# Attention on one Trainium2 core: the weighted sums in runs of three key blocks, the next minimum and exponential ahead of the evictions

## Chip, cores and metric

The kernel runs on one core of a Trainium2 chip. The metric is the device time of one execution in microseconds (us), lower is better. An execution of the kernel before takes 633.66 us (median of three: 632.58, 633.66 and 633.7).

## What is computed

Three stages follow each other: an attention whose mask comes from hash buckets, a mixture of experts, and a mixer. The change lies in the attention alone:

```python
q_bits = (np.einsum('bhsd,dk->bhsk', q, proj) > 0)          # 6 bits, the same for k
mask = q_bucket[:, :, :, None] == k_bucket[:, :, None, :]
scores = scale * np.matmul(q, k.transpose(0, 1, 3, 2))       # 2 x 8 heads, 768 x 768, head size 64
scores = np.where(mask, scores, -1000000000.0)
scores = scores - np.max(scores, axis=-1, keepdims=True)
attn = np.exp(scores)
attn = attn / (np.sum(attn, axis=-1, keepdims=True) + 1e-09)
return np.matmul(attn, v)
```

The attention's output is the token matrix (2 x 768 x 512) that the experts and then the mixer read.

## The kernel before

The sixteen heads are taken as eight pairs. A **unit** `u` is one head's block of 128 query rows against all 768 keys. There are 96 units (`NU`), six to a **group** `g = u // 6` (three query blocks times two heads of a pair); below `w = u % 6` is the unit's place in its group and `h = u % 2` its head. Units 0 to 23 (`NP2`) go through an older loop; the loop of this change goes over units 22 to 95.

What one unit does, by function:

- `scores(u)`: four TensorE matmuls of the operand tile `op` into a score tile `ps` (two buffers in PSUM), L242. The mask is part of the operands.
- `low(u)`: on VectorE (DVE) the scores are moved from `ps` to a tile `sc` (three buffers) with their minimum, L249.
- `expo(u)`: on ScalarE (ACT) the exponential of `sc` in place, with the row sum, L256.
- `transp(u)`: six TensorE transposes of `sc`, three into each of two PSUM tiles `pst` (a pool of two buffers, so the next unit's first three transposes need this unit's first tile, and its next three the second), L270. Two evictions take them to `pt`, the transposed weights of the group: the first half on ACT (L282), the second half on ACT in the odd units (set `relieve`) and on DVE (L284) in the even ones.
- `av(g, kb)`: the weighted sums of a whole group over key block `kb`: two matmuls, one for each head, which write 64 rows each of `pav` (L295; in the profile each is two instructions). `av_out(g)` moves the finished `pav` to `xT` on ACT (L302) and takes the reciprocal of the row sums on DVE (L304, L305).
- `av_tok(g)` turns `xT` into token rows (px, L312, and three or four DVE operations).

The order of each engine's queue is the order in which the program is written (`manual_schedule`), and each engine takes its queue in that order. In the loop, unit `u` is written as: `scores(u + 2)`; in an odd unit of groups up to 14 two `av` of the group before (so key blocks 0 and 1 in w = 1, 2 and 3 in w = 3, 4 and 5 in w = 5); in w = 5 also `av_out`; then `transp(u)`, in which `low(u + 2)` is written after the first half's eviction and `expo(u + 2)` after the second's; then `av_tok` where one is due (w = 1), and the side work planned for that unit: halving 64-bit weights to 32 bits on DVE (`narrow`, L592, L594, L596, in five units of six up to unit 73), splitting the next pair's operands on GpSimd (POOL, L174 to L181), and loads. The last group (units 90 to 95) has its own places for `av`: there two runs of three key blocks stand already.

Of the kernel before, what the change touches and what calls it, by code (L numbers as in the profile page):

```python
# [59 lines left out]
def attention(tc, nc, cst, cbf, cst_src, tri_src, cw, qkT, vt, iw_src, route, wide, errands, xh, early):  # L60
    with ExitStack() as ctx:
# [139 lines left out]
        NU = len(units)  # L201
# [3 lines left out]
        NP2 = 24  # L205
# [25 lines left out]
        def scores(u):  # L231
            i, half, qb, h = units[u]
            op = opnd[i]
            g = u // 6
            if u % 6 == 0:
                sums[g] = sm_p.tile([128, 6], F32, name="sum")
                mns[g] = sm_p.tile([128, 6], F32, name="mn")
            ps = ps_s.tile([128, 2, 512], F32, name="ps")
            c0 = 384 * half + 128 * qb
            for x, kk in ((0, 128), (2, 76)):  # L240
                for n in range(2):
                    nc.tensor.matmul(ps[:, n, :384], lhsT=op[:kk, h, x, c0:c0 + 128],  # L242
                                     rhs=op[:kk, h, x + 1, 384 * n:384 * n + 384], start=(x == 0), stop=(x == 2))
            pss[u] = ps

        def low(u):
            g, w = u // 6, 2 * units[u][2] + units[u][3]
            sc = sc_p.tile([128, S], F32, name="sc")
            nc.vector.tensor_scalar(sc.rearrange("p (a b) -> p a b", a=2), pss.pop(u)[:, :, :384], NEG, None,  # L249
                                    op0=ALU.min, op1=ALU.min, accum_out=mns[g][:, w:w + 1])  # L250
            scs[u] = sc

        def expo(u):
            g, w = u // 6, 2 * units[u][2] + units[u][3]
            sc = scs[u]
            nc.scalar.activation(sc, sc, AF.Exp, bias=mns[g][:, w:w + 1], scale=-1.0,  # L256
                                 accum_out=sums[g][:, w:w + 1])

        def transp(u):
            _, _, qb, h = units[u]  # L260
            g = u // 6
            if u % 6 == 0:
                pts[g] = [pt_p.tile([128, NB, 384], F32, name=f"pt{x}") for x in range(2)]
            sc = scs.pop(u)
            pt = pts[g][h]
            for n in range(2):
                ps = ps_t.tile([128, 512], F32, name="pst")
                for j in range(3):
                    kb = 3 * n + j
                    nc.tensor.transpose(ps[:, 128 * j:128 * j + 128], sc[:, 128 * kb:128 * kb + 128], ident)  # L270
                dst = pt[:, 3 * n:3 * n + 3, 128 * qb:128 * qb + 128]
                src = ps[:, :384].rearrange("p (a b) -> p a b", a=3)
                if u < NP2 - 2 and h == 1:
                    if n == 0:
                        low(u + 2)
                        nc.vector.tensor_copy(dst, src)
                    else:
                        expo(u + 2)
                        nc.scalar.activation(dst, src, AF.Copy)
                    continue  # L280
                if n == 0 or u in relieve:
                    nc.scalar.activation(dst, src, AF.Copy)  # L282
                else:
                    nc.vector.tensor_copy(dst, src)  # L284
                if n == 0 and u + 2 < NU:
                    low(u + 2)
            if u + 2 < NU and (u >= NP2 - 2 or h == 0):
                expo(u + 2)

        def av(g, kb, q0=0, q1=3):  # L290
            if kb == 0 and q0 == 0:
                pav[g] = ps_a.tile([128, 512], F32, name="pav")
            sl = slice(128 * q0, 128 * q1)
            for h in range(2):
                nc.tensor.matmul(pav[g][64 * h:64 * h + 64, sl], lhsT=vtile[g // 2][:, kb, 64 * h:64 * h + 64],  # L295
                                 rhs=pts[g][h][:, kb, sl], start=(kb == 0), stop=(kb == NB - 1))

        def av_out(g, q0=0, q1=3):
            if q0 == 0:
                xTs[g] = sm_p.tile([128, 384], F32, name="xT", bufs=2)  # L300
            sl = slice(128 * q0, 128 * q1)
            nc.scalar.activation(xTs[g][:, sl], pav[g][:, sl], AF.Copy)  # L302
            rs = sums[g][:, 2 * q0:2 * q1]
            nc.vector.tensor_scalar(rs, rs, 1e-9, None, op0=ALU.add)  # L304
            nc.vector.reciprocal(rs, rs)  # L305

        def av_tok(g, between=None):
            i, half = g // 2, g % 2
            b, p = pairs[i]
            px = px_tile()[:, :438].rearrange("p (t c) -> p t c", t=3)  # L310
            for x in range(3):
                nc.tensor.matmul(px[:, x], lhsT=xTs[g][:, 128 * x:128 * x + 128], rhs=iw[:, p], start=True, stop=True)  # L312
            inv = sums[g].rearrange("p (t h) -> p t h", t=3).unsqueeze(3)
            X, L = route.tiles(b)
            t = slice(3 * half, 3 * half + 3)
            lg = sm_p.tile([128, 3, 2, 9], F32, name="lg", bufs=2)
            nc.vector.tensor_tensor(lg, px[:, :, 128:].rearrange("p t (h e) -> p t h e", h=2),
                                    inv.to_broadcast([128, 3, 2, 9]), op=ALU.mult)
            Lh = L[:, t, :]
            if p == 0:  # L320
                nc.vector.tensor_tensor(Lh, lg[:, :, 0], lg[:, :, 1], op=ALU.add)
            else:
                nc.vector.tensor_tensor(Lh, Lh, lg[:, :, 0], op=ALU.add)
                nc.vector.tensor_tensor(Lh, Lh, lg[:, :, 1], op=ALU.add)
            if between is not None:
                between()
            nc.vector.tensor_tensor(
                X[:, t, 128 * p:128 * p + 128].rearrange("p t (h d) -> p t h d", h=2),
                px[:, :, :128].rearrange("p t (h d) -> p t h d", h=2),
                inv.to_broadcast([128, 3, 2, 64]), op=ALU.mult)  # L330
# [174 lines left out]
        for p in range(NP2 // 2 - 1):  # L505
            g, w = p // 3, p % 3
            scores2(p + 1)
            transp(2 * p)
            if g >= 1:
                av(g - 1, 2 * w)  # L510
                av(g - 1, 2 * w + 1)
                if w == 2:
                    av_out(g - 1)
            transp(2 * p + 1)
            for u in (2 * p, 2 * p + 1):
                for x in tok.get(u, ()):
                    av_tok(x)
                for f in todo.pop(u, ()):
                    f()
        for u in range(NP2 - 2, NU):  # L520
            g, w = u // 6, u % 6
            last = g == NG - 1
            if u + 2 < NU:
                scores(u + 2)
            if g >= 1 and not last and w % 2 == 1:
                av(g - 1, w - 1)
                av(g - 1, w)
            if w == 5 and g >= 1 and not last:
                av_out(g - 1)
            if last and w == 1:  # L530
                for kb in range(3, NB):
                    av(g - 1, kb)
                av_out(g - 1)
            if last and w in (2, 4):
                q = w // 4
                for kb in range(NB):
                    av(g, kb, q, q + 1)
                av_out(g, q, q + 1)
            transp(u)
            if last and w == 0:  # L540
                for kb in range(3):
                    av(g - 1, kb)
            for x in tok.get(u, ()):
                av_tok(x)
            for f in todo.pop(u, ()):
                f()
# [3 lines left out]
        g = NG - 1  # L550
# [860 lines left out]
def build(tc, nc, a):  # L1411
    with ExitStack() as ctx:
# [45 lines left out]
        with tc.tile_pool(name="xtok", bufs=1, side="right") as xp:  # L1458
            route = Router(nc, tc, cst, cbf, rp, xp, xs, ys)
            zt = []  # L1460

            def zero(e):
                if not zt:
                    zt.append(wr_a.tile([128, 2048], F32, name="wr"))
                    nc.gpsimd.memset(zt[0][:, :1024], 0.0)
                nc.sync.dma_start(xs[CAP * e:CAP * e + CAP].rearrange("(p r) d -> p (r d)", r=2), zt[0][:, :1024])

            errands = [lambda e=e: zero(e) for e in range(E)] + [lambda: wload(0), lambda: wload(1)]
            x0 = attention(tc, nc, cst, cbf, a["cst"], a["tri"], cw, a["qkT"], a["vt"], a["iw"], route, wide, errands,
                           xh, early)  # L1470
# [67 lines left out]
```

## Time and profile before

| | |
|---|---|
| median of three executions | 633.66 us |
| the profiled execution | 636.94 us |
| its span, first to last instruction | 635.1 us |
| TensorE (PE) busy | 620.9 us, 98% |
| DVE busy | 402.7 us, 63% |
| ACT busy | 351.4 us, 55% |
| POOL busy | 256.8 us, 40% |
| units 24 to 89 (first transposes at 68.75, last at 228.62) | 159.9 us |

Times inside the span are counted from its first instruction. PE's line shows matmuls; PEld, its weight loads, runs beside them. Ends of matmuls are modelled, so what PE's work costs is read from the distance between the starts of successive groups. A bracket behind a row gives the idle time before it and what ended that.

### The profile page before, as it was taken

The page shows a single profiled execution, that of the slowest core. Times are in us where ns is not written, and L with a number is a line of the kernel's source. Part 1 is how long each engine was busy: PE and PEld are TensorE (multiplying, and loading weights), DVE is VectorE, ACT ScalarE, POOL GpSimd, SP SyncE. Part 2 cuts the span into 40 slices and gives each one's busy share as a digit, 9 for nine tenths or more (in the row PEclk, how much of TensorE's full clock was granted, in tenths as well). Part 3 has the DMA queues.
Part 4 walks back from the last instruction along what each step waited for, and adds up shares of the span by engine and source line. Part 5 has one row for each costly group of instructions (what it writes and reads, how often), then busy time and mean ns, then how long its engine had stood idle before and what let it go on. Part 6 is the DMA issues. An engine that isn't in the chain of part 4 may idle for free. (4 is left out here: it accounts for less than half of the span.)

```text
span 635.1 us, 10543 instructions
## 1 busy us (share of the span) xinstructions
PE 620.9 (98%) x4028; PEld 498.2 (78%) x4028; DVE 402.7 (63%) x740; ACT 351.4 (55%) x643; POOL 256.8 (40%) x191
## 2 busy tenths in 40 slices
PE   8999999999989999999999999999999999999997
PEld 4666676766657767889889989989788888788896
DVE  5667788879777657737786646544456876854252
ACT  5757667767657756445455545544657457533220
POOL 2252140422340241444355453355456676774320
PEclk9999999999989999999999999999999999999999
DMA  7349999786945101788868798855223322321012
GB/s 241 102 138 279 288 297 293 194 207 220 250 141 138 50 0 64 244 322 278 309 216 299 242 326 298 261 209 183 85 84 113 103 100 84 116 84 66 35 34 100
DMA packets 51828, 112.57 MB, mean 177 GB/s; under 512 B 4112, under 2 KB 13984, under 8 KB 51776
## 3 DMA queue, kind: packets, MB, share of 16 engines
q1 hardware_dynamic: 48416, 97.73, 48.9%
q10 hardware_dynamic: 1440, 7.86, 3.6%
q0 software_dynamic: 1920, 6.29, 3.0%
q8 instruction: 32, 0.52, 0.3%
q14 instruction: 20, 0.16, 0.1%
HBM read 74.06 MB, written 22.54 MB: 152 GB/s over the span
## 5 line engine op out<-in xcount | busy, mean ns | idle before, releaser
L249 DVE TENSOR_SCALAR_CACHE_REDUCE sc<-ps 128x768 f32<-128x768 f32 x96 | 90.7, 953 | 29.1 <-PE ps L242 14.5
L1263 PE MATMUL acc<-wt,z 128*128 128x256 f32 (+1 forms) x576 | 106.4, 340 | 0.6 <-DVE z L1249 0.5
L1263 PEld LDWEIGHTS acc<-wt,z 128*128 128x128 f32 x576 | 90.5, 188 | 15.8 <-DVE z L1249 1.4
L848 POOL TENSOR_TENSOR whl<-wr,whl 128x1024 fp32r<-128x1024 f32 x30 | 72.1, 2425 | 69.6 <-ACT whl L846 62.8
L256 ACT ACTIVATE sc<-sc,mn 128x768 f32<-128x768 f32 x96 | 89.7, 936 | 14.2 <-DVE sc L249 12.7
L921 PE MATMUL mph<-xhl,whl 128*128 128x256 f32 x768 | 94.2, 284 | 0.4 <-DVE xhl L584 0.3
L921 PEld LDWEIGHTS mph<-xhl,whl 128*128 128x128 f32 x768 | 93.1, 192 | 1.3 <-DVE xhl L584 0.5
L270 PEld LDWEIGHTS pst<-cst,sc 128*128 128x128 f32 x576 | 64.1, 141 | 35.4 <-ACT sc L256 14.4
L282 ACT ACTIVATE pt<-pst 128x384 f32<-128x384 f32 x132 | 59.6, 488 | 51.1 <-PE pst L270 47.8
L270 PE MATMUL pst<-cst,sc 128*128 128x128 f32 x576 | 83.0, 280 | 3.2 <-ACT pt L282 3.1
L937 PE MATMUL mpy<-whl,h 128*128 128x512 f32 x336 | 79.4, 392 | 0.0
L295 PE MATMUL pav<-pt,v 128*64 128x384 f32 (+1 forms) x432 | 74.3, 468 | 0.0
L846 ACT ACTIVATE whl<-wr 128x1024 fp32r<-128x1024 f32 x64 | 64.0, 1051 | 15.4 <-PE mpy L937 6.5
L937 PEld LDWEIGHTS mpy<-whl,h 128*128 128x128 f32 x336 | 62.1, 188 | 12.3
L242 PE MATMUL ps<-op 128*128 128x384 f32 (+1 forms) x288 | 68.6, 360 | 0.5 <-DVE sc L249 0.5
L242 PEld LDWEIGHTS ps<-op 128*128 128x128 f32 (+1 forms) x288 | 47.2, 190 | 3.5 <-issue 2.5
L616 POOL TENSOR_TENSOR wt<-wr,wt 128x768 fp32r<-128x768 f32 x24 | 45.8, 1927 | 8.9 <-issue 3.9
L295 PEld LDWEIGHTS pav<-pt,v 128*64 128x64 f32 x432 | 26.4, 137 | 27.9 <-issue 27.7
L848 DVE TENSOR_TENSOR whl<-wr,whl 128x1024 fp32r<-128x1024 f32 x34 | 40.0, 1219 | 6.7 <-ACT whl L846 6.7
L925 DVE SCALAR_TENSOR_TENSOR h<-mph,h 128x512 fp32r<-128x512 f32 x32 | 21.7, 687 | 33.0 <-ACT h L924 33.0
L924 ACT ACTIVATE h<-mph 128x512 fp32r<-128x512 f32 x32 | 19.1, 596 | 42.6 <-PE mph L921 41.1
L1289 PE MATMUL bk<-u,wch 128*128 128x512 f32 (+1 forms) x192 | 35.0, 339 | 0.8 <-DVE u L1279 0.8
(190 smaller groups left out, 823.0 us busy)
## 6 DMA issues: line engine op xcount, KB each, us to landing
wr<-w SPq DMA_DIRECT2D x32, 1024.0 KB
op<-hl SPq DMA_DIRECT2D x36, 384.0 KB
wr<-wtf ACTq DMA_DIRECT2D x10, 768.0 KB
w<-wt SPq DMA_DIRECT2D x16, 384.0 KB
rqk<-qkT SPq DMA_DIRECT2D x7, 768.0 KB
xs<-wr SPq DMA_DIRECT2D x8, 512.0 KB
xi<-xs SPq DMA_DIRECT2D x7, 512.0 KB
ys<-y SPq DMA_DIRECT2D x7, 512.0 KB
```

Source lines behind the costliest of these rows:

```text
L242: nc.tensor.matmul(ps[:, n, :384], lhsT=op[:kk, h, x, c0:c0 + 128], rhs=op[:kk, h, x + 1, 384 * n:384 * n + 384], start=(x == 0), stop=(x ...
L249: nc.vector.tensor_scalar(sc.rearrange("p (a b) -> p a b", a=2), pss.pop(u)[:, :, :384], NEG, None, op0=ALU.min, op1=ALU.min, accum_out=mn ...
L256: nc.scalar.activation(sc, sc, AF.Exp, bias=mns[g][:, w:w + 1], scale=-1.0, accum_out=sums[g][:, w:w + 1])
L270: nc.tensor.transpose(ps[:, 128 * j:128 * j + 128], sc[:, 128 * kb:128 * kb + 128], ident)
L282: nc.scalar.activation(dst, src, AF.Copy)
L295: nc.tensor.matmul(pav[g][64 * h:64 * h + 64, sl], lhsT=vtile[g // 2][:, kb, 64 * h:64 * h + 64], rhs=pts[g][h][:, kb, sl], start=(kb == 0 ...
L616: self.nc.gpsimd.tensor_tensor(t[:, 1, r], raw[:, sl], t[:, 0, r].bitcast(F32), op=ALU.subtract)
L846: nc.scalar.activation(t[0][:, sl], raw[:, sl], AF.Copy)
L848: lo.tensor_tensor(t[1][:, sl], raw[:, sl], t[0][:, sl].bitcast(F32), op=ALU.subtract)
L921: nc.tensor.matmul(ps[:, ff], lhsT=w[a][:, w0:w0 + 128], rhs=x[:, bb, k], start=(n == 0), stop=(n == 23))
L937: nc.tensor.matmul(yps[e][n], lhsT=h[:, a, fo, 128 * n:128 * n + 128], rhs=w[bb][:, 512 * f:512 * f + 512], start=(fo == 0 and q == 0), st ...
L1263: nc.tensor.matmul(span(b, d, t0, n), lhsT=z[:, a, r, 128 * d:128 * d + 128], rhs=w[:, bb, r, t0:t0 + n], start=(t == 0 and i == 0 and (d ...
```

## The change

In units 24 to 89 the weighted sums are written three key blocks at a time, in w = 2 (blocks 0 to 2) and w = 5 (blocks 3 to 5), where two at a time stood in w = 1, 3 and 5. In these same units (`u % 3 == 2`) `low(u + 2)` and `expo(u + 2)` are written ahead of the transposes and of both evictions; elsewhere they stay where they were.

```diff
             sc = scs.pop(u)
             pt = pts[g][h]
+            ahead = NP2 <= u < NU - 6 and u % 3 == 2
+            if ahead:
+                low(u + 2)
+                expo(u + 2)
             for n in range(2):
                 ps = ps_t.tile([128, 512], F32, name="pst")
...
-                if n == 0 and u + 2 < NU:
+                if n == 0 and u + 2 < NU and not ahead:
                     low(u + 2)
-            if u + 2 < NU and (u >= NP2 - 2 or h == 0):
+            if u + 2 < NU and (u >= NP2 - 2 or h == 0) and not ahead:
                 expo(u + 2)
...
             if u + 2 < NU:
                 scores(u + 2)
-            if g >= 1 and not last and w % 2 == 1:
-                av(g - 1, w - 1)
-                av(g - 1, w)
+            run = 2 if g < NP2 // 6 else 3
+            if not last and w % run == run - 1:
+                for kb in range(w + 1 - run, w + 1):
+                    av(g - 1, kb)
             if w == 5 and g >= 1 and not last:
                 av_out(g - 1)
```

ScalarE's queue around the end of group 4, before: the eviction of unit 28 (pt0_1101, head 0) and an exponential, then unit 29 (w = 5): xT, its two evictions (pt1_1102) and an exponential, then the eviction of unit 30 (pt0_1260).

```order
L282 ACTIVATE pt0_1101<-pst_1214 128x3x128
L256 ACTIVATE sc_1219,sum_1207<-sc_1219,mn_1208 128x768
L302 ACTIVATE xT_1237<-pav_1126 128x384
L282 ACTIVATE pt1_1102<-pst_1241 128x3x128
L282 ACTIVATE pt1_1102<-pst_1248 128x3x128
L256 ACTIVATE sc_1246,sum_1207<-sc_1246,mn_1208 128x768
L282 ACTIVATE pt0_1260<-pst_1262 128x3x128
```

The same place of ScalarE's queue with the change (lines 4 higher):

```order
L286 ACTIVATE pt0_1101<-pst_1212 128x3x128
L256 ACTIVATE sc_1217,sum_1205<-sc_1217,mn_1206 128x768
L306 ACTIVATE xT_1237<-pav_1155 128x384
L256 ACTIVATE sc_1241,sum_1205<-sc_1241,mn_1206 128x768
L286 ACTIVATE pt1_1102<-pst_1244 128x3x128
L286 ACTIVATE pt1_1102<-pst_1249 128x3x128
L286 ACTIVATE pt0_1260<-pst_1262 128x3x128
```

The exponential moved from behind the two evictions of unit 29 to between xT and them. On TensorE, units 27 to 29 of the kernel before: scores, weighted sums in units 27 and 29, transposes.

```order
L295 MATMUL pav<-pt_925,v 64x384
L295 MATMUL pav<-pt_926,v 64x384
L295 MATMUL pav<-pt_925,v 64x384
L295 MATMUL pav<-pt_926,v 64x384
L270 MATMUL pst<-cst,sc 128x128 x6
L242 MATMUL ps<-op 128x384 x4
L270 MATMUL pst<-cst,sc 128x128 x6
L242 MATMUL ps<-op 128x384 x4
L295 MATMUL pav<-pt_925,v 64x384
L295 MATMUL pav<-pt_926,v 64x384
L295 MATMUL pav<-pt_925,v 64x384
L295 MATMUL pav<-pt_926,v 64x384
```

And the same three units with the change:

```order
L242 MATMUL ps<-op 128x384 x4
L274 MATMUL pst<-cst,sc 128x128 x6
L242 MATMUL ps<-op 128x384 x4
L274 MATMUL pst<-cst,sc 128x128 x6
L242 MATMUL ps<-op 128x384 x4
L299 MATMUL pav<-pt_925,v 64x384
L299 MATMUL pav<-pt_926,v 64x384
L299 MATMUL pav<-pt_925,v 64x384
L299 MATMUL pav<-pt_926,v 64x384
L299 MATMUL pav<-pt_925,v 64x384
L299 MATMUL pav<-pt_926,v 64x384
L274 MATMUL pst<-cst,sc 128x128 x6
```

Unit 27 (w = 3) has no weighted sums any more, and unit 29 (w = 5) has six matmuls of them in a row where it had four.

## Rows read from the trace of the kernel before

**Rows 1.** The page: busy time, share of the span and instructions of each engine

```profile
PE 620.9 (98%) x4028; PEld 498.2 (78%) x4028; DVE 402.7 (63%) x740; ACT 351.4 (55%) x643; POOL 256.8 (40%) x191
```

**Rows 2.** Windows: us, each engine's busy time (instructions), granted clock, DMA share, GB/s

```profile
80.00:120.00 40.00, 39.46 (x261) 28.66 (x261) 31.67 (x76) 28.51 (x63) 8.24 (x9) 1.00 1.02 280
120.00:160.00 40.00, 40.00 (x275) 27.32 (x272) 34.04 (x79) 28.37 (x63) 12.12 (x11) 1.00 0.72 202
...
177.00:182.00 5.00, 4.42 (x17) 2.19 (x18) 4.80 (x7) 2.70 (x6) 4.92 (x4) 0.67 0.47 185
```

**Rows 3.** Waits of TensorE, 68 to 229 us: total, times, longest

```profile
PE pst L270 <- ACT pt L282: 2.4, 2, 1.5
PE ps L242 <- DVE sc L249: 0.5, 1, 0.5
```

**Rows 4.** Timeline of TensorE, 104 to 114 us: start, us, engine, line, operation

```profile
105.53 1.51 PE L295 MATMUL pav<-pt,v 128*64 128x384 f32 x8
106.97 0.87 PE L270 MATMUL pst<-cst,sc 128*128 128x128 f32 x6
107.60 0.94 PE L242 MATMUL ps<-op 128*128 128x384 f32 x4
108.38 0.82 PE L270 MATMUL pst<-cst,sc 128*128 128x128 f32 x6
108.96 0.94 PE L242 MATMUL ps<-op 128*128 128x384 f32 x4
109.83 1.51 PE L295 MATMUL pav<-pt,v 128*64 128x384 f32 x8
111.27 0.87 PE L270 MATMUL pst<-cst,sc 128*128 128x128 f32 x6
...
112.69 0.82 PE L270 MATMUL pst<-cst,sc 128*128 128x128 f32 x6
```

**Rows 5.** Timeline of TensorE, 228 to 240 us

```profile
234.53 2.16 PE L295 MATMUL pav<-pt,v 128*64 128x384 f32 x12
236.62 0.87 PE L270 MATMUL pst<-cst,sc 128*128 128x128 f32 x6
```

**Rows 6.** Timeline of ScalarE, 110.5 to 114 us

```profile
111.39 0.49 ACT L302 ACTIVATE xT<-pav 128x384 f32<-128x384 f32 x1 [0.69 <-PE pav L295]
111.86 0.87 ACT L282 ACTIVATE pt<-pst 128x384 f32<-128x384 f32 x2
112.61 0.94 ACT L256 ACTIVATE sc<-sc,mn 128x768 f32<-128x768 f32 x1
...
113.53 0.49 ACT L282 ACTIVATE pt<-pst 128x384 f32<-128x384 f32 x1
```

**Rows 7.** Timeline of all engines, 66 to 70 us

```profile
68.22 0.86 ACT L282 ACTIVATE pt<-pst 128x384 f32<-128x384 f32 x2
...
68.75 0.93 PE L270 MATMUL pst<-cst,sc 128*128 128x128 f32 x6
...
69.44 0.78 PE L242 MATMUL ps<-op 128*128 128x384 f32 x3
```

**Rows 8.** Timeline of VectorE, at 92, 110 and 181 us

```profile
92.08 2.23 DVE L596 SCALAR_TENSOR_TENSOR w<-w,w 128x384 uint32<-128x384 uint32 x1
94.24 0.94 DVE L249 TENSOR_SCALAR_CACHE_REDUCE sc<-ps 128x768 f32<-128x768 f32 x1
...
110.60 0.95 DVE L249 TENSOR_SCALAR_CACHE_REDUCE sc<-ps 128x768 f32<-128x768 f32 x1
111.48 0.55 DVE L594 SCALAR_TENSOR_TENSOR w<-w,w 128x384 uint32<-128x384 uint32 x1
...
181.22 1.28 DVE L594 SCALAR_TENSOR_TENSOR w<-w,w 128x384 uint32<-128x384 uint32 x1
```

**Rows 9.** Timeline of TensorE, 172 to 183 us

```profile
173.09 0.87 PE L270 MATMUL pst<-cst,sc 128*128 128x128 f32 x6
...
181.52 1.16 PE L270 MATMUL pst<-cst,sc 128*128 128x128 f32 x6
```

## The prediction

> **What bounds the kernel now.** I read the page's busy times first: TensorE (PE) is busy for 98% of the span [rows 1]. A busy share says little by itself, so next the windows and the waits: in the stretch of the change PE has 39.46 of 40 us and 40.00 of 40 us of work [rows 2], and in all of units 24 to 89 only three of its groups waited, 2.9 us together [rows 3]. So the order of PE's queue sets the time, and a microsecond more or less there moves the end: after the attention, PE's share of the span leaves next to no idle time in which a shift could vanish. The timeline of PE then gives the price of each piece by the distance from start to start [rows 4]: weighted sums of two key blocks 1.44 us (105.53 to 106.97), transposes behind them 0.63, scores ahead of transposes 0.78, transposes behind scores 0.58, scores ahead of weighted sums 0.87. Two units are 4.30 us (106.97 to 111.27).
>
> The profiled execution is 636.94 us, 3.3 above the median of 633.66. It holds one event of about that size: from 173.09 to 181.52 two units took 8.43 instead of 4.30 us, without a cause that the rows name [rows 9]. I carry it as it is and lay the change on both: the sum is a difference, and I give the time against the median.
>
> **Fewer, longer runs: 3.1 us less.** A run of three key blocks stands in the last group already: 234.53 to 236.62, 2.09 us [rows 5], against 1.44 for two. So two runs of three cost 4.18 and three runs of two 4.32: 0.14 less in a group. One unit in a group loses its run: its scores cost 0.78 in place of 0.87 and its transposes 0.58 in place of 0.63, 0.14 more. That is 0.28 in each of groups 4 to 14, eleven of them: 3.1 us. PE does nothing else that is new; no instruction is added or taken away on any engine, and no DMA moves past another on SP's or POOL's queue.
>
> **The minimum ahead of the evictions: nothing by itself.** On DVE the order stays as it was: the minimum stood ahead of DVE's own eviction before. It needs only the scores that were written just ahead of the run, and the run of 2.09 us covers its 0.95 [rows 8].
>
> **The exponential ahead of the evictions: 8.0 us more.** In w = 2 it is free: ScalarE would be idle during the run, and does the exponential there. In w = 5 it isn't, because `av_out` is written ahead of `transp`. ScalarE's queue there was xT, two evictions, exponential; now it is xT, exponential, two evictions. xT waits for the end of the run, so the exponential can't use the run: it starts after xT, and the evictions start after it. Before, xT started 0.12 after the transposes (111.27 [rows 4], 111.39 [rows 6]), the evictions 0.47 after xT; the exponential holds the queue for 0.92 (112.61 to 113.53) [rows 6]. The first eviction now starts 0.12 + 0.47 + 0.92 = 1.51 after the transposes and ends 0.49 later [rows 6], at 2.00. The next unit's first transposes want the PSUM tile that it empties, and would start 1.42 after these (111.27 to 112.69) [rows 4]. That this tile binds, and how sharply, one place before the change shows: evictions start at 68.22, the first is through after 0.49, and the next transposes start at 68.75, 0.04 behind it; the second half waits as well, so that these transposes take 0.69 to the next scores in place of 0.58 [rows 7, 4]. So PE stands for 2.04 - 1.42 = 0.62, and then for 0.11: 0.73 us in each of eleven groups, all units w = 5 from 29 to 89, 8.0 us. Before, the first eviction ended 1.08 after the transposes, with 0.3 to spare, which is why this queue costs nothing now. After the wait PE is 0.73 later, and the rest of the engines have that much more room.
>
> Bounds: no less than the first half alone, 0.62 x 11 = 6.8; no more than the exponential's 0.92 in full, 10.1, if the spare time is gone through a late xT.
>
> **Late minima: 1.0 us more.** Scores write a tile that the minimum of two units earlier must have left. Before, such scores stood 4.30 us apart everywhere; now, after two units without a run, 2.72 (twice 0.78 + 0.58) once in three units. Scores and minimum take 0.87 + 0.95 of it, so DVE may be late by 0.9 us there, and could be by 2.5. DVE is late where its 32-bit halving meets POOL's splitting: five rows from 2.23 (92.08) to 1.28 us (181.22) in place of 0.55 [rows 8]. One of them cost PE 0.54 before: the 0.5 of [rows 3] ends with the minimum of 94.24. I take 1.0 for the five together, between nothing and their whole excess of about 6.
>
> The sum: -3.1 + 8.0 + 1.0 = +5.9 us. Against the median 639.6 us, against the profiled execution 642.8.
>
> **Rivals.** *A, the other side: only the longer runs count.* Then the time is 633.66 - 3.1 = 630.6. It decides at w = 5: the eviction's end must come within 1.42 us of the transposes' start. For it speaks that PE's own price falls by rows of this trace; against it the exponential between xT and the evictions, whose sum passes 1.42 by 0.6. The Trainium skill says, in TensorEngine Tiling (Array Packing), Key Properties, that a change of tiling mode drains TensorE; by that rule alone, with the two heads in halves of the array, fewer runs are fewer drains and A is the outcome. The trace agrees with a price of 0.28 a group for the changes of kind, and shows no row of the drain itself. Chance 0.10.
>
> *B: DVE binds in earnest.* All of the excess of the five long rows reaches PE: 633.66 - 3.1 + 8.0 + 5.5 = 644.1 (6.0 less the 0.5 that is paid already). Against it: most of them lie where a run follows and gives the time back. Chance 0.13.
>
> *C: the run of three costs what two plus one cost,* because the last group, which gave its price, has other neighbours: no gain, 633.66 + 8.0 + 1.0 = 642.7. Chance 0.06.
>
> *D: part of the wait is hidden.* If something else on PE (side work in w = 5) fills half of it, the sum is -3.1 + 4.0 + 1.0 = +1.9, 635.6; with less than that no change can be measured. For it speaks nothing in the rows but the few units with side matmuls. Chance 0.08, half of it within 0.2%.
>
> *E: the clock.* After PE's two longest waits, 2.4 us together [rows 3], the granted clock was 0.67 over 177 to 182 us, so at the lower level, 1.2 GHz, for part of it; after the single wait of 0.5 it stayed at 1.00, the 2.4 GHz [rows 2]. Eleven waits of 0.73 are nearer to the second. If each cost what a fall may have cost there, at most the 4.1 us of [rows 9], the time would be 639.6 + 11 x 4.1 = 684.7. The Trainium skill, in TensorE: Matmul & The Clock Gate, A second HAM failure mode: psum-queue depth-cycling, tells of a kernel whose short pauses at its PSUM buffers made the clock swing between its levels; that speaks against this change. The trace's one wait of 0.5 us doesn't show it. Chance 0.02.
>
> **How the numbers follow.** The forecast has 0.61 and gives the time, 639.6; its own range is 637.4 (wait at 6.8, no late minimum) to 642.5 (wait at 9.4, that is 0.85 a group, and 2.5 of late minima). The range reaches to D below and towards B above: 635.3 to 644.5, which leaves out A, E, the half of D that is nearer to no change and the far end of B. A measurement of this kernel tells 0.2% from no change, about 1.3 us: faster is A, 0.10; same is half of D and a little of the edges, 0.05; slower is the rest, 0.85.
>
> **What would show it.** Right: PE's waits by ScalarE's evictions (transposes) rise from 2 to 11 or more, each near 0.6 us, each right behind a unit with xT; ScalarE there shows xT, exponential, two evictions without idle time; run to transposes is 2.09, and the pieces of units without a run 0.78 and 0.58; the windows of the attention show ScalarE and DVE no busier. Wrong: transposes behind w = 5 that start 1.42 after the last ones (A); scores that wait for the minimum more than three or four times (B); 2.16 or more from run to transposes (C); windows with a clock under 1.00 across the attention (E).

## The result, and the profile after

The changed kernel takes 639.83 us (median of four runs, 638.43 to 641.29), the kernel before beside it 633.41 (four runs, 632.58 to 633.7). The ratio is 1.0103, with a 95% interval of 1.0091 to 1.0115. By the ratio that is 6.5 us slower (6.4 between the medians), in the direction forecast and near the size (5.9).

Of the profiled executions (638.43 us, span 636.6, against [rows 1] and the table of before: 636.94 and 635.1) only 1.5 us of this can be seen directly, because the one of before holds the 4.1 us of [rows 9] and the one after holds no such event: 1.5 + 4.1 = 5.6. The profiled execution after is the fastest of its four; the 0.9 us between 5.6 and 6.5 stands in no trace. The page's first line, after:

```profile
PE 618.6 (97%) x4028; PEld 498.3 (78%) x4028; DVE 404.4 (64%) x740; ACT 352.2 (55%) x643; POOL 257.4 (40%) x191
```

Against [rows 1] PE is busy 2.3 us less in a span that is 1.5 longer. The instructions are the same in number, so TensorE works less and waits more. Where, the waits of TensorE show, in the stretch that holds the changed units (66 to 250 us; the columns are those of [rows 3]):

```profile
PE pst L274 <- ACT pt L286: 6.3, 13, 1.3
PE pst L274 <- DVE pt L288: 0.2, 1, 0.2
```

In [rows 3] transposes waited twice for ScalarE's evictions, both times inside the event of [rows 9] (176.16 and 177.58); now 13 times, 6.3 us together. No scores wait for a minimum any more. Next the timeline of TensorE over one whole group, from the first transposes of unit 36 (w = 0) to those of unit 42:

```profile
99.69 0.93 PE L274 MATMUL pst<-cst,sc 128*128 128x128 f32 x6 [0.38 <-ACT pt L286]
...
108.22 0.82 PE L274 MATMUL pst<-cst,sc 128*128 128x128 f32 x6
108.80 0.94 PE L242 MATMUL ps<-op 128*128 128x384 f32 x4
109.67 2.16 PE L299 MATMUL pav<-pt,v 128*64 128x384 f32 x12
111.76 0.88 PE L274 MATMUL pst<-cst,sc 128*128 128x128 f32 x6
112.39 0.94 PE L242 MATMUL ps<-op 128*128 128x384 f32 x4
113.72 0.93 PE L274 MATMUL pst<-cst,sc 128*128 128x128 f32 x6 [0.38 <-ACT pt L286]
114.40 0.94 PE L242 MATMUL ps<-op 128*128 128x384 f32 x4
115.18 0.82 PE L274 MATMUL pst<-cst,sc 128*128 128x128 f32 x6
115.83 0.41 PE L316 MATMUL px<-iw,xT 128*128 128x146 f32 x2
```

The run of three is 2.09 (109.67 to 111.76), transposes behind it 0.63, scores 0.78 and transposes 0.58 in the unit without a run (114.40 to 115.18, 108.22 to 108.80): the prices that the prediction took from [rows 4, 5]. What is new is the bracket at 113.72. The transposes of w = 0 start 1.96 behind those of w = 5 (111.76), where it was 1.42 in [rows 4], and take 0.68 to the scores (114.40) in place of 0.58. ScalarE over the same moment:

```profile
111.88 0.49 ACT L306 ACTIVATE xT<-pav 128x384 f32<-128x384 f32 x1 [1.21 <-PE pav L299]
112.26 0.93 ACT L256 ACTIVATE sc<-sc,mn 128x768 f32<-128x768 f32 x1
...
113.18 0.86 ACT L286 ACTIVATE pt<-pst 128x384 f32<-128x384 f32 x2
```

This is the queue of the prediction: xT, the exponential, then two evictions, without idle time after xT; in [rows 6] the evictions stood right behind xT. The evictions start 1.42 behind the transposes of w = 5; the first takes 0.49 [rows 6], to 113.67, and the transposes that want its tile start at 113.72.

A whole group (99.69 to 113.72) takes 14.03 us. The timeline of TensorE of the kernel before has, one group apart:

```profile
101.90 0.88 PE L270 MATMUL pst<-cst,sc 128*128 128x128 f32 x6
...
115.57 0.88 PE L270 MATMUL pst<-cst,sc 128*128 128x128 f32 x6
```

115.57 - 101.90 = 13.67. So an ordinary group is 0.36 longer. Without the waits of 0.54 and 0.10 it would be 13.39, which is 0.28 shorter than before: both terms of the sum can be read in one group. Eleven such groups would give 4.0 us; ten have the regular wait, as experiment 6 will show, which gives 3.3. The rest stands in groups that are not ordinary: of the 11 waits behind a w = 5, eight are 0.38 like the one above (the bracket counts from the modelled end of the scores, 112.39 + 0.94, so it shows less than the 0.54 from start to start), three are longer (0.51, 0.94, 1.28), and two more stand behind a w = 2. One of the long ones, timelines of all engines:

```profile
121.45 1.95 POOL L181 TENSOR_TENSOR hl<-rqk,hl 128x768 fp32r<-128x768 f32 x1
121.63 0.94 DVE L249 TENSOR_SCALAR_CACHE_REDUCE sc<-ps 128x768 f32<-128x768 f32 x1
...
122.50 1.32 DVE L599 SCALAR_TENSOR_TENSOR w<-w,w 128x384 uint32<-128x384 uint32 x1
...
123.70 2.16 PE L299 MATMUL pav<-pt,v 128*64 128x384 f32 x12
123.74 0.94 DVE L249 TENSOR_SCALAR_CACHE_REDUCE sc<-ps 128x768 f32<-128x768 f32 x1
...
125.09 0.54 DVE L601 SCALAR_TENSOR_TENSOR w<-w,w 128x384 uint32<-128x384 uint32 x1
...
125.79 0.88 PE L274 MATMUL pst<-cst,sc 128*128 128x128 f32 x6
125.85 0.95 DVE L249 TENSOR_SCALAR_CACHE_REDUCE sc<-ps 128x768 f32<-128x768 f32 x1
125.90 0.49 ACT L306 ACTIVATE xT<-pav 128x384 f32<-128x384 f32 x1
...
126.85 0.94 ACT L256 ACTIVATE sc<-sc,mn 128x768 f32<-128x768 f32 x1 [0.46 <-DVE sc L249]
...
127.78 0.85 ACT L286 ACTIVATE pt<-pst 128x384 f32<-128x384 f32 x2
...
128.31 0.93 PE L274 MATMUL pst<-cst,sc 128*128 128x128 f32 x6 [0.94 <-ACT pt L286]
```

Read from the top: POOL splits operands (121.45, 1.95 long), the halving beside it (122.50) takes 1.32 and not 0.54 as at 125.09, and DVE's queue behind it is late: a minimum at 123.74, an eviction, another halving, and at 125.85 the minimum of the unit two ahead, when the run of three (123.70) that should have covered it is over. The exponential waits 0.46 for it, from the end of xT (125.90 + 0.49) to 126.85; the two evictions stand behind the exponential, at 127.78, and TensorE waits 0.94 at 128.31. So a late minimum no longer reaches TensorE through the scores; it reaches it through the exponential, and the evictions behind that. The longest wait, behind unit 71, goes by a longer way:

```profile
186.44 0.94 ACT L256 ACTIVATE sc<-sc,mn 128x768 f32<-128x768 f32 x1 [3.06 <-DVE X L331]
...
189.49 0.93 PE L274 MATMUL pst<-cst,sc 128*128 128x128 f32 x6 [1.28 <-ACT pt L286]
```

Here the exponential of the unit before waited for an operation of VectorE on the token rows (X), which stood behind a halving of 2.12 us (181.87); xT, the next exponential and the evictions were late with it. So "late minima" below means what VectorE's lateness costs by either way.

### The profile page after: what moved, and what is told of

Read it like the earlier page. It is cut to its first block, busy times and chain, and to the rows that moved or that the text cites. A ratio compares the mean times of both kernels' runs of the same rounds, so it can differ in the third digit from the quotient of the medians.

```text
span 636.6 us, 10543 instructions
## 1 busy us (share of the span) xinstructions
PE 618.6 (97%) x4028; PEld 498.3 (78%) x4028; DVE 404.4 (64%) x740; ACT 352.2 (55%) x643; POOL 257.4 (40%) x191
## 5 line engine op out<-in xcount | busy, mean ns | idle before, releaser
L299 PE MATMUL pav<-pt,v 128*64 128x384 f32 (+1 forms) x432 | 70.5, 459 | 0.0
```

## The experiments

All times are medians, all ratios are against the kernel before in the same set of runs (633.21, 633.07 and 633.66 us in the three sets), with their 95% interval. The theory: ScalarE's order in w = 5 costs 0.64 us in each group, the longer runs give 3.1 in all, late minima make the rest. The rivals: the longer runs cost or give nothing (C), or VectorE is the bound (B).

### 1. The order ahead in w = 2 alone

```diff
-            ahead = NP2 <= u < NU - 6 and u % 3 == 2
+            ahead = NP2 <= u < NU - 6 and u % 6 == 2
```

> The runs of three stay, and the minimum and exponential go ahead of the evictions in w = 2 alone; in w = 5 ScalarE's queue is again xT, two evictions, exponential. Queue theory (the exponential between xT and the evictions costs 0.64 us in each of eleven groups, as the changed kernel's transposes show, 1.96 in place of 1.42 and 0.68 in place of 0.58): the 7.0 us go, the 3.1 of the longer runs stay, and of the late minima at most 1: 630.3 to 631.5 us, 0.995 to 0.997 of before, transposes behind w = 5 at 1.42. DVE theory (late minima make the loss): still above 637. Theory that the run of three costs PE as much as it saves: 633 to 634.

Measured: 633.83 (eleven runs), 1.0009 [1.0, 1.0017]. Its waits of TensorE by ScalarE's evictions are 1.3 us in 2. Undoing the order in w = 5 takes 0.94% off the changed kernel, 6.0 us: the loss is in w = 5. But the time is 2.3 us above the expected range and inside the one of the third theory (633 to 634), so the gain of the longer runs does not come out in full. Experiment 3 shows where a part of it stays.

### 2. xT behind the exponential in w = 5

`av_out` written after `low(u + 2)` and `expo(u + 2)`, so that the exponential can use the run of three while xT waits for its end:

```diff
             if ahead:
                 low(u + 2)
                 expo(u + 2)
+                if u % 6 == 5:
+                    av_out(g - 1)
...
-            if w == 5 and g >= 1 and not last:
+            if w == 5 and g >= 1 and not last and u < NP2:
                 av_out(g - 1)
```

> As the changed kernel, but xT and the reciprocals are written behind the minimum and exponential of w = 5, so that ScalarE does the exponential during the run, then xT, then the two evictions. Queue theory: as in the run with w = 2 alone or a little better, since the exponential is out of the way sooner: 630.0 to 631.0 us, 0.994 to 0.996 of before. DVE theory: still above 637, as DVE's queue hardly changes. Theory that the run of three saves nothing: 633 to 634.

Measured: 636.83 (six runs), 1.0057 [1.0038, 1.0076]. A miss: more than half of the loss stays. The waits of TensorE, 66 to 250 us:

```profile
PE pst L276 <- ACT pt L288: 4.8, 5, 1.6
PE ps L242 <- DVE sc L249: 0.7, 1, 0.7
```

There are five waits for evictions instead of 13, four of them behind a w = 5, but the longest is 1.6 us. The regular wait is gone and the irregular ones have grown, since an exponential that waits for its minimum now holds up xT as well as the evictions (at the longest the exponential waited 1.07 us for VectorE and started at 128.24, xT at 129.18, the evictions at 129.55).

### 3. The longer runs alone

```diff
-            ahead = NP2 <= u < NU - 6 and u % 3 == 2
+            ahead = False
```

> The runs of three alone: minimum and exponential stay behind the evictions everywhere. Queue theory: no wait at w = 5; 630.3 to 632 us, with up to 1 us lost where a unit without a run is near its end on ScalarE. If the exponential ahead in w = 2 is needed for the longer runs: 632 to 634, with waits of transposes behind w = 2.

Measured: 632.62 (twelve runs), 0.9989 [0.9976, 1.0002]: 0.7 us better, where 3.1, less up to 1, were expected, and not to be told from no change. The time lies in the range of the other theory (632 to 634), but no transposes wait behind a w = 2 as that theory asks. The timeline of TensorE, one group (unit 42, w = 0, to unit 48) and two waits:

```profile
112.43 0.82 PE L274 MATMUL pst<-cst,sc 128*128 128x128 f32 x6
...
113.83 0.94 PE L274 MATMUL pst<-cst,sc 128*128 128x128 f32 x6
114.60 0.91 PE L316 MATMUL px<-iw,xT 128*128 128x146 f32 x6
...
125.96 0.82 PE L274 MATMUL pst<-cst,sc 128*128 128x128 f32 x6
127.39 0.97 PE L242 MATMUL ps<-op 128*128 128x384 f32 x4 [0.61 <-DVE sc L249]
128.83 0.88 PE L274 MATMUL pst<-cst,sc 128*128 128x128 f32 x6 [0.47 <-ACT pt L286]
```

112.43 to 125.96 is 13.53, so 0.14 better than before's 13.67 and not 0.28. The pieces are as priced, but one: the transposes of w = 1 (113.83), which used to have a run ahead of them, take 0.77 to the token matmuls (px, 114.60), where the changed kernel has 0.65 (115.18 to 115.83). Their second half wants the tile that VectorE evicts, and there the eviction (113.61) stands behind a minimum (112.73); in the changed kernel everything behind w = 5 is late by half a microsecond on TensorE, and this wait lies inside it. That is 0.14 x 11 = 1.5 us; the waits of 0.61 and 0.47 (a minimum behind two long halvings) make 1.1 more. 633.2 - 3.1 + 1.5 + 1.1 = 632.7 is near the 632.62 measured. It is a rough account: it leaves out the 0.5 that the kernel before waits for a minimum [rows 3].

### 4. The order ahead alone, with runs of two

```diff
-            run = 2 if g < NP2 // 6 else 3
+            run = 2
```

> Minimum and exponential ahead in every third unit, with the runs of two where they were (w = 1, 3 and 5). Queue theory: the run's end still holds xT and the exponential behind it in w = 5, 0.64 us in each of eleven groups, and nothing is saved: 633.4 + 7.0 = 640.4 us, 1.009 to 1.013 of before. DVE theory: between 633 and 635, because scores are 4.30 us apart again. Theory that the run of three costs: 633 to 635 too.

Measured: 644.57 (five runs), 1.0182 [1.0161, 1.0203]. The loss is there without the longer runs, and with them the same order is 0.79% (5.0 us) cheaper, which speaks against C, though it is not the price of the runs alone: here w = 2 has no run beside the exponential ahead. The loss is 4 us larger than was expected. The waits of TensorE:

```profile
PE pst L274 <- ACT pt L286: 7.3, 13, 1.2
PE pst L274 <- DVE pt L288: 1.8, 2, 0.9
```

Here the waits reach 1.2 us too, and the two waits for VectorE's evictions, each followed by one of 0.36 for ScalarE's, stand behind a w = 2: 2.5 us of the 4. That with a run of only two key blocks a minimum in w = 5 has less cover would explain the rest, but is not shown.

### 5 to 7. The same three kernels with two of three halvings left out

The theory that late minima make the difference to the sum asks for kernels in which fewer minima are late. In these, 32 of the 48 halving operations are left out, everything else stays:

```diff
-            narrow_ops(nc, w32[m], w64[m].rearrange("p (n two) -> p n two", two=2), j - 1)
+            if j == 1:
+                narrow_ops(nc, w32[m], w64[m].rearrange("p (n two) -> p n two", two=2), j - 1)
```

The kernel before, so lightened:

> The kernel before, with two of the three operations that halve each 64-bit weight in the attention left out (32 of 48; the weights of the mixer are then not those of the reference). It is the base for the two runs beside it. Where late minima cost the kernel before only the 0.5 us that its trace shows: 632.5 to 633.2 us. If DVE costs it more than shows: below 632.

Measured: 632.5 (twelve runs), 0.9994 [0.9981, 1.0007].

The changed kernel, so lightened:

> The changed kernel with the same 32 operations left out. Theory that the change's loss is a queue part (0.64 x 11 = 7.0 us), less 3.1 for the longer runs, and the rest late minima behind the halving: the rest goes, base + 3.9 to 4.5, some 637 us, against 639.8 with the operations. Theory that late minima come from the token operations and the routing on DVE instead: base + 6, as before.

Measured: 635.84 (five runs), 1.0041 [1.0028, 1.0055]. Its waits of TensorE, and the first and the last of the ten in the timeline:

```profile
PE pst L274 <- ACT pt L286: 3.8, 10, 0.4
...
PE ps L242 <- DVE sc L249: 0.3, 1, 0.3
```

```profile
85.22 0.93 PE L274 MATMUL pst<-cst,sc 128*128 128x128 f32 x6 [0.38 <-ACT pt L286]
...
229.51 0.93 PE L274 MATMUL pst<-cst,sc 128*128 128x128 f32 x6 [0.38 <-ACT pt L286]
```

Ten waits of exactly 0.38, each behind a w = 5, and none longer. That is the part of the loss that hangs on ScalarE's order alone. The eleventh place has no wait: behind the transposes of unit 71 stand token matmuls, and the next transposes start 2.16 behind them (184.97 to 187.13), as in the kernel before (2.17, 191.93 to 194.10). So the regular price is 0.64 x 10 = 6.4 us, and less the 3.1 of the longer runs it is 3.3. Expected were 3.9 to 4.5 above the lightened kernel before; the two medians lie 3.3 apart.

The changed kernel loses 0.62% (3.9 us) more with all halvings than with a third of them, the kernel before 0.06% (0.4): late minima cost the changed kernel some 3.5 us by the medians. By the profiles, from the transposes of unit 24 to those of unit 89, it is 2.1: 68.90 to 229.56 against 68.97 to 227.56.

The longer runs alone, so lightened:

> The runs of three alone, minimum and exponential in their old places, with the same 32 operations left out. Theory that late minima behind the halving ate the gain of the longer runs: base - 2.6 to - 3.1, some 630.0 us. Theory that the run of three doesn't save 0.28 a group: base - 0.8 as with the operations, some 632.

Measured: 630.12 (five runs), 0.9949 [0.9936, 0.9962], so 0.45% or 2.9 us under the lightened kernel before; by the ends of the two intervals between 1.2 and 4.5. The rows give 1.5: its groups too take 13.53, with the 0.14 at w = 1. Between the two profiled executions, from unit 24 to unit 90, it is 1.8 (68.65 to 223.81 against 68.97 to 225.90). The longer runs give something, and the ratio alone does not say whether 1.5 or 3.1.

### 8. Halvings moved beside the runs

If only late minima keep the longer runs from paying, halvings two at a time in w = 2 and 5, with the order as before, could pay:

```diff
-        free = [u for u in range(16, NU) if u % 6 != 1 and u not in busy]
+        free = [u for u in range(16, NP2) if u % 6 != 1 and u not in busy]
+        free += [u for u in range(NP2, NU - 6) if u % 3 == 2 for _ in range(1 if u in busy else 2)]
```

> The runs of three alone, all halving operations kept, but from unit 24 on they are written two at a time into the units with a run (w = 2 and w = 5, to unit 89), where DVE has the run's 2.09 us to catch up, and none into the units without one. Theory of late minima behind the halving: most of the gain comes back, 630.0 to 631.3 us, 0.995 to 0.997 of before. Rival: two halving operations in one unit meet POOL's splitting together and delay the next minimum as much: 632 to 633.5.

Measured: 651.86 (five runs), 1.0286 [1.0272, 1.03]. A failure, for two reasons. The waits of SP's queue and of TensorE, 66 to 250 us:

```profile
SPq L396 <- DVE w L598: 46.1, 5, 13.5
```

```profile
PE ps L242 <- DMA op<-bt: 5.6, 2, 3.8
PE ps L242 <- DVE sc L249: 5.6, 3, 2.6
...
PE ps L242 <- DMA op<-hl: 1.4, 1, 1.4
```

A halving's loads and stores go with it. SP, in whose queue the loads of the operands stand too, waited 46.1 us at L396 for halvings (a wait that the longer runs alone don't have), the operands came late, and scores waited for them (5.6 and 1.4 us). The other reason is the rival that was named before the run, two halvings that meet POOL's splitting together:

```profile
92.89 1.83 DVE L600 SCALAR_TENSOR_TENSOR w<-w,w 128x384 uint32<-128x384 uint32 x1
94.75 2.04 DVE L602 SCALAR_TENSOR_TENSOR w<-w,w 128x384 uint32<-128x384 uint32 x1
```

Behind these two halvings, scores waited 2.6 us for a minimum, the longest of the three such waits (5.6 together).

### 9. xT behind the exponential, with two of three halvings left out

Experiment 2 with the edit of experiments 5 to 7, to see whether its remaining loss is the late minima:

> The kernel with xT behind the exponential in w = 5, and with 32 of the 48 halving operations left out as in the light runs before it. It differs from the light run of the changed kernel (635.8 us) only in ScalarE's order of xT and exponential. Queue theory: ten to eleven waits of 0.64 us go and, with minima on time, nothing takes their place: 629.0 to 630.0 us, like the light run with runs of three alone (630.1), and no wait of transposes behind w = 5. If the eviction behind the exponential costs even where xT isn't in the way: 632 to 634.

Measured: 631.35 (twelve runs), 0.9968 [0.9957, 0.9979]. The waits for evictions, 66 to 250 us:

```profile
PE pst L276 <- ACT pt L288: 0.4, 1, 0.4
```

None of the ten behind a w = 5 is left; the one that there is stands behind a w = 2. The time is still 1.4 us above the expected range. Against experiment 6, which differs only in where xT stands in ScalarE's queue, this is 0.73% less, 4.6 us, where the regular price is 6.4. And with all halvings (experiment 2) it is 0.89% more, 5.6 us: in this order late minima cost most of all.

### 10 and 11. Halvings in w = 4 and 1

Three of the four halvings of a group in w = 4, one in w = 1, where no minimum that stands ahead is near; once with the order as before, once with xT behind the exponential:

```diff
-        free = [u for u in range(16, NU) if u % 6 != 1 and u not in busy]
+        free = [u for u in range(16, NP2) if u % 6 != 1 and u not in busy]
+        free += [u for u in range(NP2, NU - 6) for _ in range((0, 1, 0, 0, 3, 0)[u % 6])]
```

> Runs of three alone, all halving operations kept, from unit 24 on three of them in w = 4 and one in w = 1, so that the next minima behind them are those that are written into a unit with a run; the loads and stores of the weights go one unit around them on SP's queue. Theory of late minima: a run of 2.09 us takes up three halving operations (1.65 us), and most of the 3.1 comes back: 630.3 to 631.5 us. Rival, as in the run before with two in w = 2 and w = 5 (651.9): SP's queue waits for the halving and the operands of the next pair come late: above 634.

> The kernel with xT behind the exponential, with the halving operations placed as in the run beside it. If the minima that are written into units with a run come late by the three halving operations, this kernel pays more than the one beside it, since the exponential ahead of the evictions waits for just these minima: 632 to 637. If they are on time: 630 to 631, like the run beside it.

Measured: 637.65 (six runs), 1.0078 [1.0059, 1.0098], and 645.88 (five runs), 1.0198 [1.0175, 1.0221]. Both lose. The second has twelve waits for evictions, up to 1.8 us:

```profile
PE pst L276 <- ACT pt L288: 9.8, 12, 1.8
```

Behind three halvings in w = 4 the minimum of w = 5 is late in ten of the eleven groups, and xT, exponential and evictions are late with it. What the first loses was settled in part only. In its profiled execution, the fastest of its six at 635.65, TensorE waits 1.3 us for minima, 1.2 for ScalarE's evictions and 0.9 for an operation of the routing (erow) that VectorE does late, against 0.6, 0.5 and nothing in experiment 3. That is 2.3 more, and the spans of the two are 2.4 apart (633.8 and 631.4). No wait there is for operands. The other executions are longer the lower their mean granted clock is: 636.77 at 1.000, 636.88 at 0.999, 638.42 at 0.998, 638.95 at 0.996, 640.23 at 0.995.

No version beat both kernels with the computation whole: the longer runs alone (experiment 3) come nearest, and can't be told from the kernel before.

## Why the prediction came out as it did

**What bounds the kernel: right.** Each microsecond that TensorE's queue gained or waited in the attention moved the end: 4.92 us from unit 24 to unit 89 (160.66 against 159.87 with the 4.1-us event) and 0.54 behind it, 5.5 together, against 5.6 between the profiled executions.

**Fewer, longer runs: right in the changed kernel.** 0.28 a group is there, 13.67 against 13.39 plus waits. Alone, the longer runs gave half of it in the rows (experiment 3); the prediction had not seen that the run ahead of w = 1 also covered an eviction of VectorE there. In the changed kernel the longer wait behind w = 5 covers it again.

**The exponential ahead of the evictions in w = 5: right in mechanism, a little too large.** 0.64 us in ten groups, 6.4, for 0.73 in eleven and 8.0. Behind unit 71 the token matmuls fill the wait, a small D that the sum had left out. In the other groups the step that was off is "the evictions 0.47 after xT", taken over for the exponential: it started 0.38 after xT (111.88 to 112.26), so the first eviction came 1.42 after the transposes and not 1.51. Experiment 1 (6.0 us back), experiment 4 (the loss without longer runs) and the pair 6 and 9 (4.6 us by the place of xT alone, and none of the ten waits left) show the cause.

**The minimum ahead of the evictions, and the exponential in w = 2: nearly nothing, not nothing.** Two waits of 0.25 and 0.30 stand behind units w = 2, where a minimum was late. Experiments 1 and 3 differ in this order alone, and lie 0.2% (1.3 us) apart; in experiment 1 a wait of 0.9 stands behind a w = 2, in experiment 3 none.

**Late minima: the step that failed.** The prediction put 1.0 us on them, through scores that refill a tile 2.72 apart. What the regular part of 3.3 leaves is 6.5 - 3.3 = 3.2 by the ratio and 5.6 - 3.3 = 2.3 between the profiled executions; experiment 6 against the changed kernel says 3.5 by the medians and 2.1 by the profiles. And the way was another: not one group of scores waited for a minimum in the changed kernel. VectorE's lateness delayed the exponential, and this the evictions, which the edit had put behind it. The prediction counted ScalarE's new order at its regular price only, and did not ask what happens to the evictions when the minimum is late. The two errors, 1.6 too much and 1.1 to 2.5 too little, nearly cancel: that the forecast came so near to the result is partly luck.

**The rivals.** A (630.6) is out: the transposes behind w = 5 never started 1.42 after the last ones where nothing else stood between. The drain of the Trainium skill's TensorEngine Tiling (Array Packing), Key Properties, on which A could rest, agrees with the 0.28 a group that fewer runs gave, though no row shows the drain itself; 0.28 is less than half of the 0.64 that the waits take. C is out by the 2.09 of each run. B holds in part: late minima cost more than the forecast had, less than the 5.5 of B, and by another way. (The excess of the five long rows behind B is 4.9 by the trace, not 6: 2.23, 2.12, 0.84, 1.15 and 1.28 in place of 0.55.) E did not occur. The windows after:

```profile
80.00:120.00 40.00, 38.61 (x254) 27.56 (x253) 31.26 (x73) 27.82 (x60) 9.46 (x10) 1.00 0.98 276
120.00:160.00 40.00, 38.00 (x258) 26.49 (x255) 32.62 (x75) 27.33 (x61) 10.49 (x10) 1.00 0.67 184
160.00:200.00 40.00, 38.22 (x267) 28.41 (x266) 32.30 (x79) 28.43 (x61) 13.14 (x16) 1.00 0.68 184
```

Through pauses of up to 1.3 us the granted clock stayed at 1.00, the 2.4 GHz, in each of these windows, and the four executions had means of 0.999 and 1.000. The failure that the Trainium skill tells of in TensorE: Matmul & The Clock Gate, A second HAM failure mode: psum-queue depth-cycling, a clock that swings with short pauses at PSUM buffers, did not show in this kernel.

**Open:** the 0.9 us between the profiled executions and the ratio, and what lowers the clock in some executions of experiment 10.

## What to carry to other kernels

When an operation is moved ahead in an in-order queue so that it can use a wait, look at what else stands in front of it: here xT was waiting for the same run that the exponential should have used, and the regular price came straight from the written order. Everything that is put behind the moved operation inherits its lateness, not only its length, so ask what the operation itself waits for when it is late. And side work that is shifted to make room takes its transfers along, past others in the same DMA queue, and meets other engines' work in its new place.

## What was not expected of the hardware

The mean granted clock is lower in single executions of kernels whose other executions keep it. The profiled execution of before, 636.94, has a mean of 0.997; in the last set of runs, 17 of the 18 executions of the kernel before had 0.999 or 1.000 and took 631.91 to 634.43, the one at 0.997 took 636.57. The prediction carried the event of [rows 9] without a cause. Windows of the kernel before show its order (columns as in [rows 2]):

```profile
174.00:178.00 4.00, 1.62 (x11) 1.07 (x10) 0.81 (x1) 1.46 (x3) 3.67 (x6) 1.00 0.86 290
...
179.00:182.00 3.00, 3.00 (x10) 1.01 (x9) 3.00 (x4) 0.74 (x2) 3.00 (x2) 0.50 0.13 51
```

First TensorE waited, 1.51 and 0.87 us at a clock of 1.00, with VectorE and ScalarE idle for most of the time too. The clock of 0.50, the 1.2 GHz, came behind that, and one run of two key blocks took 2.76 (178.76 to 181.52) in place of 1.44. So more than half of the 4.1 us is the waits, and the fall is most of the rest. What held up all three engines is not shown; the changed kernel's profiled execution has no such event. In the kernel of experiment 8, where TensorE waited up to 3.8 us, all five executions had means of 0.986 to 0.992.

An operation's start-to-start distance depends on what follows: ScalarE's xT took 0.47 to an eviction [rows 6], 0.38 to an exponential.

A halving of VectorE (0.55 by itself [rows 8]) beside POOL's splitting seems to wait for the end of POOL's instruction, and not to run at a lower rate: the one at 122.50 ended at 123.82, 0.42 behind the end of the split at 123.40, and in the kernel before the one at 92.08 [rows 8] ended at 94.31, 0.41 behind the end of a split at 93.90. The Trainium skill says, in SBUF — State Buffer, Who interferes with whom, that a VectorE instruction with two SBUF inputs contends with a GpSimd instruction that reads SBUF, and that the port pair they share is an exclusive lock; these rows agree. The minimum of 121.63, which reads PSUM, kept its 0.94 beside the same split.
